# Reads of transposed probabilities moved from SyncE's queue to ScalarE's, in an attention and MLP kernel

## The chip, the cores and the metric

The kernel runs on one core of a Trainium2 chip. The metric is the device time of one execution in microseconds (us). The core has five engines with an instruction queue each: TensorE (PE in the profile; its weight loads are PEld), VectorE (DVE), ScalarE (ACT), GpSimd (POOL) and SyncE (SP). Each takes its own instructions strictly in order; they meet through semaphores. SP and ACT can also issue DMAs, which run on 16 DMA engines.

## The reference

```python
# 8 batches, 8 heads, 576 positions, head size 64
scores = q @ k.transpose(0, 1, 3, 2) / sqrt(64)
rel = pos[:, None] - pos[None, :]
slopes = 2.0 ** (-8.0 * (arange(8) + 1) / 8)
mask = (rel >= 0) & (rel < 128)
scores = where(mask, scores - slopes * abs(rel), -1e9)
attn = exp(scores - max(scores)); attn /= sum(attn) + 1e-9
x = (attn @ v)                      # then laid out as [4608 tokens, 512]
out = relu(x @ w_in) ** 2 @ w_out   # w_in 512 x 2048, w_out 2048 x 512
```

Attention with a sliding window of 128 positions feeds a two-layer MLP. All is float32; the MLP's products are made of high and low parts in a rounded format (fp32r), three matmuls for one.

## The kernel before

The 4608 tokens are nine chunks of 512 (`c`), each with four pairs of heads (`p`). A pair of heads of a chunk is a `Couple` (number `q`), made of two `Segment`s of 256 tokens (number `k`, from 0 to 71). A first part of the program (`start`) loads and converts the weights and does segments 0 to 15 and the MLP of the first chunk. Then `middle` does the rest. From some 250 us on, the first MLP layer uses Strassen-like sums of weights: seven products `M1, M5, M6, M2, M7, M3, M4` for two blocks (step number `n`). Their weights were written to HBM as `ws` between 137 and 250 us and are streamed back as tiles named `flow`. The second layer (`part`, line 388, `acc`) fills the room between them. PE's order is written out by hand.

Into this order 28 "visits" are put, one for each couple. A visit (`Visit`) does on PE: `one` and `two`, which multiply the previous couple's probabilities with the values (line 743, tile `pp`), and between them `scores` of the new couple (line 756).

Between two visits the new couple goes through softmax, segment by segment: copies and masks (`base`, `fold`), maxima (`t`, line 422), exponentials on ACT (`e`, line 429), sums, normalization on POOL (`norm`, line 441, tile `t`). Then the probabilities must be transposed. `Segment.squares` does so in four steps, which carry the change:

- `square` (line 493): DVE transposes squares of 32 x 32 into the tile `pp`.
- `write` (line 497): SP issues four DMAs of 64 KB that put the squares into a DRAM tile `way`.
- `read` (line 502): SP waits until the writes have landed and issues one DMA of 256 KB that reads `way` back into `pp` in the order wanted.
- `before` and `same` (line 508): POOL waits for the read and masks the two halves with `affine_select`.

The visit that uses the couple starts with `one`, which waits for `same` of both segments. Its second half `two` also waits for a no-operation on POOL (line 760). So a segment is late for its visit if this line of square, write, read and masks ends after PE gets there.

All loads, stores of results (`send`), streams of weight sums (`flow`) and spills of weight sums (`ws`) go through `bulk` (line 123) on SP's queue, as do `write` and `read`. For segments 16 to 27 (`k < CALM`), `read` leaves its DMA in `K.quiet`, and the next `bulk` then waits until that read has landed.

The order of the instructions on all engines but PE comes from a planner (`Plan`) when the program is built. Each step has an engine, an estimated duration, predecessors, a due time, and a `lag` that is added after its predecessors. The planner walks through a model of time and takes the ready step with the lowest due time. A step handed over from SP counts 2.0 us more, one from ACT 0.15. `DUE` holds the due times and `LAG` lags of the weight sums' steps. In the model, `quiet` and `calm` (2.4 us) hold bulk transfers after a read.

The drains of the seven products gate PE: `M6` waits for `s1` (ACT, line 339), `M2` for `R` (ACT, line 341), `M7` for `s2` (ACT, line 343), and the next `M1` needs the bank that `C21` (ACT, line 351) empties.

Of the kernel before, what the change touches and what calls it, by code (L numbers as in the profile page):

```python
# [55 lines left out]
CALM = 28  # L56
# [8 lines left out]
class Kern:  # L65
# [251 lines left out]
    def chain(self):  # L317
        if "one" not in self.open:
            self.banks("one", "two")
        self.P = self.pools[0].tile([128, 512], F32, name="chain")[:, 0:256]  # L320

# [11 lines left out]
    def seven(self, n):  # L333
# [3 lines left out]
        return {  # L337
            "M1": lambda: (self.chain(), self.product(n, 0, self.P, "B11", True)),
            "s1": lambda: nc.scalar.copy(four[0][:, one], self.P),
            "M5": lambda: (self.rest(), self.product(n, 1, self.R, "T1", True)),  # L340
            "R": lambda: nc.scalar.copy(four[1][:, two], self.R),
            "M6": lambda: self.product(n, 2, self.P, "T2"),
            "s2": lambda: nc.scalar.copy(four[0][:, two], self.P),
            "M2": lambda: self.product(n, 3, self.Q, "B21"),
            "C11": lambda: add(four[0][:, one], self.Q),
            "M7": lambda: self.product(n, 4, self.P, "T3"),
            "C22": lambda: add(four[1][:, two], self.P),
# [63 lines left out]
class Segment:  # L411
# [76 lines left out]
    def squares(self):  # L488
        nc = self.nc
        self.place()  # L490
        at = lambda x, pattern: x.rearrange("p m c -> p (m c)").rearrange(pattern, m=4, c=32)
        squares = at(self.prev, "p (b m c) -> p b m c")
        nc.vector.transpose(squares.rearrange("p b m c -> p m b c"), self.t.rearrange("p m (b c) -> p m b c", c=32))
        yield
        way = self.K.dr.tile([128, 512], F32, name="way")
        for a in range(4):
            nc.sync.dma_start(
                way.rearrange("(b r) (a f) -> a r b f", r=32, a=4)[a],
                squares[32 * a : 32 * a + 32].rearrange("r b m c -> r b (m c)"),
            )  # L500
        yield
        made = nc.sync.dma_start(self.own.rearrange("p m c -> p (m c)"), way)
        if self.K.calm and self.k < CALM:
            self.K.quiet = made
        self.own, self.prev = (at(x, "p (a m c) -> p a m c") for x in (self.own, self.prev))
        for to, sign, op in ((self.prev, 1, ALU.is_gt), (self.own, -1, ALU.is_ge)):
            yield
            nc.gpsimd.affine_select(  # L508
                to, self.own, pattern=[[-32 * sign, 4], [0, 4], [-sign, 32]], compare_op=op, fill=0.0,
                base=0, channel_multiplier=sign,  # L510
            )
# [327 lines left out]
class Plan:  # L839
# [5 lines left out]
    def add(self, name, engine, us, after, due, do, take=None, free=None, lag=0):  # L845
        rooms = lambda r: (r,) if isinstance(r, str) else r or ()
        assert name not in self.steps, name
        self.steps[name] = (engine, us, after, due + NUDGE.get(name, 0), do, rooms(take), rooms(free), lag)
# [64 lines left out]
def start(K):  # L913
# [109 lines left out]


ACT, DVE, POOL = "Activation", "DVE", "Pool"
LAG = {"a0": 5, "r0": 1, "s2": 5.5, "h0": 2.5, "l0": 0.5, "w0": 1.5}
DUE = {
    "wait": (0.3, 1), "give": (-49.7, -45.4, -56.8, -41.1), "send": (-5.5,), "load": (57.9, 14.5), "fill": (4.1, 12.2),
    "base": (-95.4, -1.6), "fold": (14.4, 18.6), "t": (-148.1, -124.5), "e": (17.7, -22), "sum": (-74.4, -18.5),
    "norm": (-66.5, -66.6), "square": (30.1, -17.8), "first": (-800, -48.8, 17.5, -51.6),  # L1030
    "ws": (25.9, 40.9, 61, 100.6, 76, 70.4, 79.8, 124.2), "flow": (30, 32.6), "sq": (26, 47.2), "high": (-48.4, -45.6),
    "hl": (-116.2, -92.7), "early": (73.8, 75.3, 94.3, 88.6, 30.9, 76.9),
    "third": (40.7, 35.4, 25.2, 18.2, -9.2, 3.5, 49.5, 31.9, 9.4, 18.2, -0.2, 26.2),
    "last": (-6.5, -34.8, -6.1, 24.6, -34.4, -48, -21.5, 14.7, -26.2, -11.8, -33.6, -11.8),
}
SOFT = dict(M1=0.72, g=0.7, first=2.79, one=0.85, scores=0.75, two=0.65)
PIECES = ("M1", "M5", "M6", "M2", "M7", "M4", "M3")
# [6 lines left out]


def middle(K, waiting):
    P = Plan(DUE["wait"][0], ("t", "ws"), DUE["wait"][1], 4.3, 2.4)
    for name, n in (
        ("one", 1), ("two", 1), ("s", 1), ("t", 1), ("pp", 2), ("qk", 2), ("v", 1), ("o", 4), ("hh", 1), ("r", 1),
    ):  # L1050
# [2 lines left out]
    now, last = 0.0, ()  # L1053

    def pe(name, us, after, fn, take=None, free=None):
        nonlocal now, last
        P.add(name, "PE", us, tuple(after) + last, now, fn, take, free)
        now, last = now + us, (name,)
        return now
# [15 lines left out]
    def chain(q, s, V):  # L1075
        G, k = waiting[q].both[s], 2 * q + s
        n = lambda a, *m: (a, k, *m)
        for m in range(4):
            P.add(n("t", m), DVE, 0.22, (n("t", m - 1) if m else n("fold"),), V + DUE["t"][s], do(G.top, m))
            P.add(n("e", m), ACT, 0.4, (n("t", m),) + ((n("e", m - 1),) if m else ()), V + DUE["e"][s], do(G.exp, m))  # L1080
        P.add(n("sum"), DVE, 0.38, (n("e", 3),), V + DUE["sum"][s], G.sums)
        P.add(n("norm"), POOL, 1.1, (n("sum"),), V + DUE["norm"][s], G.norm)
        turned(q, s, V + DUE["square"][s], (n("norm"),))

    def turned(q, s, d, after):
        G, k = waiting[q].both[s], 2 * q + s
        n = lambda a, *m: (a, k, *m)
        step = do(next, G.squares(), None)
        P.add(n("square"), DVE, 0.72, after, d, step, "pp", "t")
        P.add(n("write"), "SP", 1.8, (n("square"),), d - 500, step)  # L1090
        P.add(n("read"), "SP", 0.7, (n("write"),), d - 500, step, None, None, 2)
        P.add(n("before"), POOL, 0.81, (n("read"),), d - 500, step)
        P.add(n("same"), POOL, 0.81, (n("before"),), d - 500, step)

    def visit(q):
# [52 lines left out]
    for s in range(2):  # L1148
        turned(8, s, 4.0 + 3 * s, ())
    for n in range(NF, 2 * NF):  # L1150
        g = K.gemm1(*divmod(n, NF))
        step = lambda g=g: next(g, None)
        if n == NF:
            second(2)
        t = pe(("first", n), SOFT["first"], (), step, ("one", "two"))
# [8 lines left out]
        if n % 2:  # L1164
# [3 lines left out]
            step = lambda g=g: next(g, None)  # L1168
            w = lambda a: ("ws", j, a)
            d = t + DUE["ws"][j]  # L1170
            after = (("first", n),)
            early = (("first", max(NF, n - 5)),)
# [4 lines left out]
            before = ()  # L1177
            for name, engine, us, after in todo:
                lag = LAG.get(name, 0)
                P.add(  # L1180
# [3 lines left out]
                before = (w(name),)  # L1184
# [22 lines left out]
    for n in range(NF, FULL):  # L1207
        c, j = divmod(n, 8)
# [5 lines left out]
        for names, count in zip((("M1",), ("M5", "M6"), ("M2", "M7"), ("M3", "M4")), counts):  # L1214
            for m in names:
# [3 lines left out]
                t = pe((m, n), SOFT["M1"], after, steps[m], {"M1": "one", "M5": "two"}.get(m))  # L1219
# [12 lines left out]
        for f in range(2):  # L1232
            g = K.squared(n, f)
            step = lambda g=g: next(g, None)
# [22 lines left out]
@with_exitstack  # L1257
def tile_attn_moe(ctx: ExitStack, tc: tile.TileContext, *aps):
    K = Kern(ctx, tc, *aps)
    K.const()  # L1260
    with tc.manual_schedule(engines={ENGINES["PE"]}):
        with tc.manual_schedule(engines={e for n, e in ENGINES.items() if n != "PE"}):
            start(K)
            K.join(ctx)
            K.rooms()
            middle(K, {8: K.pairs[8]})
# [58 lines left out]
```

## Time and the profile before

| | |
|---|---|
| median of 3 runs | 915.62 us (913.82 to 916.09) |
| profiled execution | 915.75 us, of which the profile's span is 914.0 us |
| granted TensorE clock | 0.999 |
| PE busy | 903.4 us, 99% of the span |
| weight loads busy | 800.5 us, 88% |
| DVE, ACT, POOL busy | 581.8, 467.0, 260.2 us |
| DMA | 212.95 MB, 233 GB/s in the mean |
| DMA issues of the four steps | 256 writes `way<-pp` of 64 KB, 64 reads `pp<-way` of 256 KB, all on SP |

Busy time is the share in which an engine executes. For PE it is modelled from the starts of matmuls, so the idle time that the waits show is the safer measure. A row of waits names who waited, for whom, the total, the number of times and the longest. The time of a DMA "to landing" is counted from its issue.

### The profile page before, as it was taken

What the parts mean: (1) busy time and instruction counts of PE and PEld (TensorE: products, weight loads), DVE (VectorE), ACT (ScalarE), POOL (GpSimd) and SP (SyncE); (2) the same over time, 40 slices, a digit from 0 to 9 for tenths busy, and PEclk for the clock granted to TensorE, in tenths of its full rate; (3) what the DMA queues carried; (4) which work ended last, traced back from release to release, by engine and by line L of the source; (5) the groups of instructions that cost most, each with busy time, mean ns of one, the idle gap of its engine ahead of it and who ended that gap; (6) DMA issues with size and microseconds to landing.
All of it is one profiled execution on the core that took longest, in us unless ns stands there. A gap on an engine that the chain in (4) does not pass through costs nothing.

```text
span 914.0 us, 23218 instructions
## 1 busy us (share of the span) xinstructions
PE 903.4 (99%) x8500; PEld 800.5 (88%) x8500; DVE 581.8 (64%) x1596; ACT 467.0 (51%) x1321; POOL 260.2 (28%) x339
## 2 busy tenths in 40 slices
PE   8999999999999999999999999999999999999998
PEld 5688888888899998999999999999999989989997
DVE  6999882667776666665656665667666566653333
ACT  7898663566554445444544444445444454432222
POOL 4213335665422322213222322231322221230000
PEclk9999999999999999999999999999999999999999
DMA  9985326768888878777877778777977786667541
GB/s 343 403 313 171 88 62 218 236 215 270 292 285 297 295 248 283 233 237 239 256 236 246 245 242 290 233 230 213 294 231 221 245 248 192 197 208 221 172 127 47
DMA packets 137569, 212.95 MB, mean 233 GB/s; under 512 B 15217, under 2 KB 49393, under 8 KB 137457
## 3 DMA queue, kind: packets, MB, share of 16 engines
q1 hardware_dynamic: 137024, 210.96, 71.1%
q8 instruction: 68, 1.11, 0.5%
q10 hardware_dynamic: 432, 0.52, 0.2%
q14 instruction: 45, 0.36, 0.1%
HBM read 170.52 MB, written 40.89 MB: 231 GB/s over the span
## 4 chain that ended last, share of the span: by engine, by line
PE 90%; DMA 7%; DVE 1%; POOL 1%; ACT 1%; SPq 1%; issue 0%; POOLq 0%; DVEq 0%; ACTq 0%
PE acc L388 42%; PE chain L331 16%; PE rest L331 12%; PE g L233 9%; PE s L743 5%; PE g L756 2%; DMA raw<-in_dram 2%; DMA pp<-way 1%; PE s L756 1%; DMA qk<-in_dram 1%; DMA flow<-ws 1%; PE at L520 1%; POOL pp L508 1%; DMA wide<-in_dram 1%; DMA out_dram<-o 0%
## 5 line engine op out<-in xcount | busy, mean ns | idle before, releaser
L388 PE MATMUL acc<-hh,w 128*128 128x512 f32 x1152 | 405.8, 398 | 0.0
L388 PEld LDWEIGHTS acc<-hh,w 128*128 128x128 f32 x1152 | 225.8, 196 | 39.3 <-issue 5.5
L388 PE MATMUL acc<-hl,w 128*128 128x512 f32 x576 | 227.7, 395 | 0.0
L336 DVE TENSOR_TENSOR four<-four,rest 128x256 f32<-128x256 f32 x112 | 47.2, 421 | 215.6 <-PE rest L331 214.5
L508 POOL TENSOR_SCALAR_AFFINE_SELECT pp<-pp 128x512 f32<-128x512 f32 x128 | 96.6, 757 | 223.8 <-DMA pp<-way 134.6
L331 PEld LDWEIGHTS rest<-xu,flow 128*128 128x128 f32 x1008 | 143.9, 191 | 13.0
L351 ACT COPY four<-chain 128x256 f32<-128x256 f32 x56 | 20.9, 373 | 251.6 <-PE chain L331 251.6
L331 PE MATMUL chain<-tees,flow 128*128 128x256 f32 x1008 | 147.6, 283 | 0.0
L331 PE MATMUL rest<-xu,flow 128*128 128x256 f32 x1008 | 146.8, 282 | 0.0
L441 POOL TENSOR_TENSOR t<-t,nm 128x512 f32<-128x512 f32 x64 | 69.5, 1089 | 239.4 <-DVE nm L437 152.1
L331 PEld LDWEIGHTS chain<-tees,flow 128*128 128x128 f32 x1008 | 132.3, 192 | 0.0
L388 PEld LDWEIGHTS acc<-hl,w 128*128 128x128 f32 x576 | 113.1, 196 | 12.6
L429 ACT ACTIVATE t<-t,nm 128x128 f32<-128x128 f32 x256 | 100.3, 394 | 9.4 <-DVE nm L422 8.8
L233 PE MATMUL g<-xu,w 128*128 128x512 f32 x384 | 95.3, 397 | 0.8 <-ACT r L242 0.8
L233 PEld LDWEIGHTS g<-xu,w 128*128 128x128 f32 x384 | 76.5, 210 | 13.8 <-ACT r L242 1.2
L422 DVE CUSTOM_DVE_ANT_0 t<-t,cst 128x128 f32<-128x128 f32 x256 | 63.1, 303 | 1.7
L251 DVE TENSOR_TENSOR hl<-r,hh 128x512 fp32r<-128x512 f32 x32 | 29.1, 910 | 42.3 <-ACT hh L249 42.2
L743 PE MATMUL s<-pp,v 64*64 64x128 f32 (+1 forms) x1792 | 53.6, 248 | 1.8 <-POOL pp L508 1.6
L656 DVE COPY_PREDICATED t<-cst,s 64x256 f32<-64x256 int32 x100 | 44.5, 445 | 12.6 <-PE s L743 5.8
L331 PEld LDWEIGHTS chain<-xu,flow 128*128 128x128 f32 x336 | 48.7, 196 | 4.0
L331 PE MATMUL chain<-xu,flow 128*128 128x256 f32 x336 | 49.4, 284 | 0.0
L429 ACT ACTIVATION_READ_ACCUMULATOR t<-t,nm 128x1 f32 x256 | 48.3, 189 | 0.0
(106 smaller groups left out, 1135.5 us busy)
## 6 DMA issues: line engine op xcount, KB each, us to landing
flow<-ws SPq DMA_DIRECT2D x392, 256.0 KB, 4.1
raw<-in_dram SPq DMA_DIRECT2D x32, 512.0 KB, 8.7
way<-pp SPq DMA_DIRECT2D x256, 64.0 KB, 2.1
pp<-way SPq DMA_DIRECT2D x64, 256.0 KB, 2.9
qk<-in_dram SPq DMA_DIRECT2D x32, 320.0 KB, 4.7
v<-in_dram SPq DMA_DIRECT2D x32, 320.0 KB, 3.6
qk<-in_dram SPq DMA_DIRECT2D x38, 256.0 KB, 5.0
out_dram<-o SPq DMA_DIRECT2D x35, 256.0 KB, 3.5
```

Source lines behind the costliest of these rows:

```text
L233: nc.tensor.matmul(g, w, xs[cc][:, part], start=i == 0, stop=i == 11)
L251: nc.vector.tensor_tensor(hl, r, hh.bitcast(F32), op=ALU.subtract)
L331: self.nc.tensor.matmul(to, w, x, start=start and k == 0, stop=k == 5, skip_group_check=True)
L336: add = lambda to, x: nc.vector.tensor_tensor(to, to, x, op=ALU.add)
L388: self.nc.tensor.matmul(self.acc[m], w, h, start=(f == 0 and i == 0), stop=(f == NF - 1 and i == 2))
L422: self.nc.vector.tensor_tensor_reduce(self.t[:, m], self.t[:, m], self.K.nrel(2 * self.p + m // 2), -0.125, BIG, ALU.add, ALU.min, self.nm ...
L429: return self.nc.scalar.activation(self.t[:, m], self.t[:, m], AF.Exp, bias=nm[:, 4 + m : 5 + m], scale=-1.0, accum_out=nm[:, m : m + 1],)
L441: self.nc.gpsimd.tensor_tensor(*(x.rearrange("p (j i) c -> p j i c", j=2) for x in (self.t, self.t)), self.rec.unsqueeze(3).to_broadcast([ ...
L508: nc.gpsimd.affine_select(to, self.own, pattern=[[-32 * sign, 4], [0, 4], [-sign, 32]], compare_op=op, fill=0.0, base=0, channel_multiplie ...
L656: nc.vector.copy_predicated(d, mask.unsqueeze(1).to_broadcast([64, 2, 2, 64]), e)
L743: yield self.nc.tensor.matmul(to, w, x, start=first and n < 2, stop=not first, skip_group_check=True)
L756: made = self.nc.tensor.matmul(to, w, x, start=not extra, stop=True, skip_group_check=True)
```

## The change

Three things. In `middle`, `read` is issued on ACT's queue; `start` keeps SP's. No read is left in `K.quiet`, so no bulk transfer waits for one. The planner's figures are new: `read` is an ACT step of 0.45 us with a lag of 1 us behind `write`, `before` has a lag of 2.4 us behind `read`, and nearly all due times and weight-sum lags differ.

```diff
@@ Segment.squares
-        made = nc.sync.dma_start(self.own.rearrange("p m c -> p (m c)"), way)
-        if self.K.calm and self.k < CALM:
-            self.K.quiet = made
+        queue = nc.scalar if self.K.calm else nc.sync
+        queue.dma_start(self.own.rearrange("p m c -> p (m c)"), way)
@@
-LAG = {"a0": 5, "r0": 1, "s2": 5.5, "h0": 2.5, "l0": 0.5, "w0": 1.5}
+LAG = {"a0": 6.5, "r0": 1.5, "s2": 4, "h0": 3, "l0": 0, "w0": 0}
 DUE = {
-    "wait": (0.3, 1), "give": (-49.7, -45.4, -56.8, -41.1), "send": (-5.5,), "load": (57.9, 14.5), "fill": (4.1, 12.2),
-    "base": (-95.4, -1.6), "fold": (14.4, 18.6), "t": (-148.1, -124.5), "e": (17.7, -22), "sum": (-74.4, -18.5),
-    "norm": (-66.5, -66.6), "square": (30.1, -17.8), "first": (-800, -48.8, 17.5, -51.6),
+    "wait": (0.3, 1), "give": (26.5, -41.3, -5.4, -21.2), "send": (-34.5,), "load": (15.5, -24.2), "fill": (-14, 18.9),
+    "base": (-67.8, -7.9), "fold": (33.1, -23.5), "t": (-141, -100), "e": (24.9, 28.8), "sum": (-60.6, -26.8),
+    "norm": (-105.2, -55.8), "square": (-10.8, -0.6), "first": (-800, -43, 44.3, -36.7),
...
 }
@@ middle
-    P = Plan(DUE["wait"][0], ("t", "ws"), DUE["wait"][1], 4.3, 2.4)
+    P = Plan(DUE["wait"][0], ("t", "ws"), DUE["wait"][1], 4.3)
@@ turned
         P.add(n("write"), "SP", 1.8, (n("square"),), d - 500, step)
-        P.add(n("read"), "SP", 0.7, (n("write"),), d - 500, step, None, None, 2)
-        P.add(n("before"), POOL, 0.81, (n("read"),), d - 500, step)
+        P.add(n("read"), ACT, 0.45, (n("write"),), d - 500, step, None, None, 1)
+        P.add(n("before"), POOL, 0.81, (n("read"),), d - 500, step, None, None, 2.4)
         P.add(n("same"), POOL, 0.81, (n("before"),), d - 500, step)
```

The diff leaves out the other due times (`ws`, `flow`, `sq`, `high`, `hl`, `early`, `third`, `last`), which change by up to some 105 us of the planner's scale. PE's order is the same before and after.

More of the change, by code (lines that the diff above doesn't have):

```diff
@@ L1025 @@
 ACT, DVE, POOL = "Activation", "DVE", "Pool"
-LAG = {"a0": 5, "r0": 1, "s2": 5.5, "h0": 2.5, "l0": 0.5, "w0": 1.5}
+LAG = {"a0": 6.5, "r0": 1.5, "s2": 4, "h0": 3, "l0": 0, "w0": 0}
 DUE = {
-    "wait": (0.3, 1), "give": (-49.7, -45.4, -56.8, -41.1), "send": (-5.5,), "load": (57.9, 14.5), "fill": (4.1, 12.2),
-    "base": (-95.4, -1.6), "fold": (14.4, 18.6), "t": (-148.1, -124.5), "e": (17.7, -22), "sum": (-74.4, -18.5),
-    "norm": (-66.5, -66.6), "square": (30.1, -17.8), "first": (-800, -48.8, 17.5, -51.6),
[L1031 to L1034, printed above, removed]
+    "wait": (0.3, 1), "give": (26.5, -41.3, -5.4, -21.2), "send": (-34.5,), "load": (15.5, -24.2), "fill": (-14, 18.9),
+    "base": (-67.8, -7.9), "fold": (33.1, -23.5), "t": (-141, -100), "e": (24.9, 28.8), "sum": (-60.6, -26.8),
+    "norm": (-105.2, -55.8), "square": (-10.8, -0.6), "first": (-800, -43, 44.3, -36.7),
+    "ws": (52.1, 52.8, 39.9, 104.3, 72.2, 74.5, 100.5, 130.1), "flow": (40.8, 46), "sq": (32.9, 20.6),
+    "high": (-112.3, -150.4), "hl": (-140.6, -122.4), "early": (58, 64.9, 63, 75.9, 48.3, 28.3),
+    "third": (75, 43.4, 37.9, 27.6, 3.4, 32, 74.1, 39.6, 11.3, 37.8, 10.5, 35.8),
+    "last": (29.7, 16.4, 29.2, 69.1, 11.7, -4, -8.1, 32.3, 1.2, 18.8, -2.1, 38.5),
 }
```

## Prediction

> **What bounds the kernel now.** I read the page first, for the engine that is full and the chain that ended last.
>
> ```profile
> PE   903.4 (99%) x8500; PEld 800.5 (88%) x8500; DVE 581.8 (64%) x1596; ACT 467.0 (51%) x1321; POOL 260.2 (28%) x339
> PE 90%; DMA 7%; DVE 1%; POOL 1%; ACT 1%; SPq 1%; issue 0%; POOLq 0%; DVEq 0%; ACTq 0%
> ```
>
> PE is full, and 90% of the chain is PE. So the change, which leaves PE's instructions and their order alone, can win only what PE idles, and can lose by making it idle more. The windows of the part that the change touches (columns: window, its length, then busy us of PE, PEld, DVE, ACT and POOL with instruction counts, clock, DMA share, GB/s) show how little that is:
>
> ```profile
> 236.00:256.00 20.00, 20.00 (x125) 18.28 (x125) 15.84 (x50) 12.18 (x38) 7.09 (x11) 1.00 0.74 231
> 256.00:353.00 97.00, 96.94 (x1024) 88.41 (x1023) 62.81 (x184) 46.64 (x149) 25.77 (x37) 1.00 0.86 282
> 353.00:450.00 97.00, 96.67 (x1013) 88.16 (x1013) 61.69 (x181) 46.09 (x142) 26.38 (x38) 1.00 0.78 245
> 450.00:741.00 291.00, 290.78 (x3067) 265.38 (x3065) 182.91 (x543) 137.62 (x431) 77.72 (x109) 1.00 0.78 247
> 741.00:816.00 75.00, 73.90 (x815) 67.26 (x813) 45.73 (x132) 34.02 (x108) 20.07 (x26) 1.00 0.67 213
> ```
>
> From 236 to 816 us PE idles 0.06 + 0.33 + 0.22 + 1.10 = 1.7 us. Then the waits of PE and of its weight loads, since a weight load stands ahead of its matmul and takes the wait first:
>
> ```profile
> PE s L743 <- POOL pp L508: 1.6, 3, 1.1
> PEld s L743 <- POOL pp L508: 2.3, 4, 1.2
> PEld s L743 <- POOLq L760: 0.4, 1, 0.4
> ```
>
> Four of 28 visits find POOL's masks (line 508) late, for 2.3 us in all, 1.2 in the worst; a fifth waits 0.4 for POOL's no-operation. The first two rows are the same four waits seen twice. So 2.3 + 0.4 = 2.7 us can be removed, and nothing else on PE depends on the reads: no row of waits has line 331 (the streams) or line 388 waiting for ACT or a DMA.
>
> Now the worst visit, at 741.2 us: the end of the square on DVE, SP's queue, POOL, ACT, PE (start, length).
>
> ```profile
> 730.36 0.70 DVE L493 STREAM_TRANSPOSE pp<-t 128x512 f32<-128x512 f32 x1
> ```
> ```profile
> 729.68 3.70 SPq L497 DMA_DIRECT2D way<-pp  x8
> 733.56 0.34 SPq L502 DMA_DIRECT2D pp<-way  x1
> 733.94 0.91 SPq L123 DMA_DIRECT2D out_dram<-o  x2
> 735.02 0.34 SPq L502 DMA_DIRECT2D pp<-way  x1
> 735.41 1.07 SPq L123 DMA_DIRECT2D out_dram<-o  x2
> 736.52 5.72 SPq L123 DMA_DIRECT2D flow<-ws  x8
> ```
> ```profile
> 736.54 1.52 POOL L508 TENSOR_SCALAR_AFFINE_SELECT pp<-pp 128x512 f32<-128x512 f32 x2 [6.62 <-DMA pp<-way]
> 740.73 1.84 POOL L508 TENSOR_SCALAR_AFFINE_SELECT pp<-pp 128x512 f32<-128x512 f32 x2 [2.67 <-DMA pp<-way]
> ```
> ```profile
> 734.99 0.37 ACT L341 COPY four<-rest 128x256 f32<-128x256 f32 x1 [0.17 <-PE rest L331]
> 735.70 0.37 ACT L343 COPY four<-chain 128x256 f32<-128x256 f32 x1 [0.34 <-PE chain L331]
> 741.36 0.37 ACT L351 COPY four<-chain 128x256 f32<-128x256 f32 x1 [5.29 <-PE chain L331]
> ```
> ```profile
> 742.62 0.89 PE L743 MATMUL s<-pp,v 64*64 64x64 f32 x29 [1.10 <-POOL pp L508]
> ```
>
> The second segment decides: its square ends at 731.06, its masks at 742.57, 11.5 us later, and PE resumes at 742.62. Of that the read's landing is the largest piece, issue at 735.02 to the masks at 740.73, 5.7 us. Two other visits just make it:
>
> ```profile
> 545.81 1.52 POOL L508 TENSOR_SCALAR_AFFINE_SELECT pp<-pp 128x512 f32<-128x512 f32 x2 [1.22 <-DMA out_dram<-o]
> 642.37 1.52 POOL L508 TENSOR_SCALAR_AFFINE_SELECT pp<-pp 128x512 f32<-128x512 f32 x2 [1.06 <-DMA pp<-way]
> ```
> ```profile
> 547.67 0.56 PE L743 MATMUL s<-pp,v 64*64 64x64 f32 x16
> 644.18 0.62 PE L743 MATMUL s<-pp,v 64*64 64x64 f32 x20
> ```
>
> Masks end at 547.33 and 643.89, so each has 0.3 us left. These six are the visits, from the fourth chunk on, that use a chunk's first pair of heads (segments 24 and 25, then every eighth). So every us by which the masks come later costs about 4 us at the four late visits and 0.7 each at these two, 5.4 us; every tenth earlier pays back at most 0.4, one tenth at each of four.
>
> **The change part by part.**
>
> *The read leaves SP.* SP no longer stops for the writes to land or, for segments 16 to 27, for the read to land:
>
> ```profile
> SPq L502 <- DMA way<-pp: 19.3, 30, 4.3
> SPq L123 <- DMA pp<-way: 15.9, 6, 3.4
> ```
>
> SP is freed of up to 35 us. Nothing on PE waits for SP's transfers, so this is worth 0 by itself; what covers it is that streams are issued well ahead of their products. But the freed SP issues its next sends and streams while the writes are still landing: at the visit above two sends and the first streams (735.41 on) can go ahead of the read instead of behind it. The first segment's read no longer queues behind the second's four writes; that moves only the first pair of masks (736.54), which does not decide: 0.
>
> *How long writes and reads then take to land.* The rows to bound it: reads of the stretch 137 to 243 us, where bulk transfers are held, and reads and writes from 360 us on, where they follow at once (min/median/max).
>
> ```profile
> L502 SPq DMA_DIRECT2D pp<-way x8: 338/338/338, 144.1 to 223.3; - x8
> DMA to landing us min/median/max: 2.5/2.7/3.0
> ```
> ```profile
> L502 SPq DMA_DIRECT2D pp<-way x38: 319/338/380, 367.4 to 808.1; - x38
> DMA to landing us min/median/max: 2.5/3.4/5.6
> ```
> ```profile
> L497 SPq DMA_DIRECT2D way<-pp x152: 302/430/1701, 363.5 to 805.8; - x152
> DMA to landing us min/median/max: 1.6/2.1/4.3
> ```
>
> Transfers issued behind a read on the same queue already cost it 3.4 - 2.7 = 0.7 us. With them ahead, and in another queue, no row shows it: from -0.7 (as if alone) to +2.2 for the read (5.6 - 3.4), and 0 to +2.2 for the write (4.3 - 2.1). I take +0.2 for both together, nearest to no change, since the same bytes share the same engines in the same few us, only in another order. The 12 reads that lose their hold get at most the 0.7; the visits from 158 to 233 us have no waits on PE and cover it.
>
> The Trainium skill ("DMA: Bandwidth & Descriptors", section "Queues, rings and completion order") says that each DMA engine takes turns between the queues it has work for, so a read in a queue of its own would not stand behind what SP queued; by that it keeps near the 2.7. The same page, "Issuing engines are not separate DMA queues", says that all queues end on the same 16 engines and only issue time is saved; by that it stays at 3.4 or more. The trace has no read on ACT's queue to decide.
>
> *The read joins ACT.* An issue there costs what the two ACT issues at the start of the program took:
>
> ```profile
> 0.81 0.44 ACTq L148 DMA_DIRECT2D wide<-in_dram  x1
> 1.28 0.45 ACTq L138 DMA_DIRECT2D cst<-in_dram  x1
> ```
>
> 56 reads of 0.44 are 25 us of ACT's queue, beside 51% busy: no bound. Per read it is +0.1 over SP's 0.34. Position: ACT is in order, so at the worst visit the read starts after the copy that ends at 735.36 or after the next at 736.07, against 735.02 on SP: +0.3 or +1.05. Before the copy of 741.36 ACT idles 5.29 us; put behind that one the read would be 6 us late, which I leave to a rival. I take +0.4 with the issue, the earlier place, since the planner puts it by time. Queued behind the waiting read are drains and casts, and PE waits for the drains. Their cover is the second layer between the products:
>
> ```profile
> 263.02 1.40 PE acc L388 x6
> ```
>
> Between a product and the one that needs its drain stand 1.40 us of this and another product (six matmuls, 0.72 in the planner's table), 2.1 less a copy of 0.37. ACT may thus stand 1.7 us for a landing before PE notices. The planner counts 3.0 us from the end of the writes' issue to the read, above the 2.1 median landing, so ACT mostly arrives late and does not stand: 0, up to +0.5 a visit if a landing takes the 4.3 and the drains follow.
>
> *The plan.* Planned from square to masks, the line was 1.8 + 2 + 0.7 + 2.0 = 6.5 us and is 1.8 + 2.0 + 1 + 0.45 + 0.15 + 2.4 = 7.8, 1.3 longer and nearer to the trace. With dues to match, squares can come up to 1.3 us earlier at the late visits. Bounds -1.3 (all fits) and 0 (DVE, busy 62.81 of 97 us in the first of these windows, has no room there); new dues can also leave another segment late, up to the +1.2 that is the longest wait now. I take -1.0.
>
> *Other dues and the weight sums' lags.* They move work that PE does not wait for (20.00 of 20.00 busy from 236 to 256): 0, covered by those margins.
>
> **Sum.** Position +0.4, landing +0.2, plan -1.0: masks 0.4 us earlier. The waits (1.2 the longest, three sharing 1.1) then keep about 0.9 of 2.3, and the no-operation's 0.4 stays: 1.4 us gained. The profiled execution took 915.75 (914.0 of span and 1.75 around it), 0.13 above the median of 915.62: 915.75 - 1.4 = 914.4.
>
> **Rivals.**
> - *All waits go.* The reads land as if alone and the squares come earlier: -2.7, 913.05. For it: four waits of at most 1.2 us against a plan that adds 1.3. Against: the same transfers share the engines. The skill's rule of turns between queues leads here: 0.7 earlier at each late visit leaves 0.5 of the longest wait.
> - *The read is late behind bulk transfers.* What SP held back goes out ahead of it. If masks come 1.0 us later, +5.4: 921.2; it decides from about 0.5 later (4 x 0.5 + 2 x 0.2 = 2.4, 918.2). For it: the landing rows (median up 0.7 from transfers merely behind, worst 5.6) and three positions on ACT that are all later than SP's. Against: the plan's 1.3.
> - *The read lands behind a drain.* A single visit of 28 with the read planned close to the copy that waits for PE (5.29 us idle) costs up to 6 us: 914.4 + 6 = 920.4. For it: ACT's long waits just ahead of the visits. Against: the planner's model knows PE's times well, as the few waits show.
> - *The move changes nothing.* The visits keep their waits: 915.7.
>
> **How the numbers follow.** A measurement here can tell about 0.3%, 2.75 us, so 912.87 to 918.37 is no difference. The forecast with its own range of 913.0 to 917.0 has 0.42, no change 0.10, all waits gone 0.25, reads late 0.18, a read behind a drain 0.05. All waits gone (913.05) stands 0.18 above the edge; the runs of before reach 1.80 below their median and 0.47 above, so I count six in ten of it as faster, 0.15, and 0.03 from the forecast's low end. Of the late reads and the drain 0.21 lie past the upper edge. So faster 0.18, same 0.61, slower 0.21. The range of 912.6 to 919.0 leaves out the worse half of the late reads and little below.
>
> **What would show it.** Right: reads on ACT's queue, no row of SP waiting at line 502 after 137 us, a sum of waits of line 743 for line 508 of about 1 us, reads landing at a median of 3.2 to 3.8. Wrong: that sum above 4 us, or waits of PE for ACT's copies (lines 339, 341, 343, 351), which are absent now; or reads at a median above 4.5.

## The result and the profile after

The changed kernel takes 944.06 us (median of 4 runs), the kernel before 915.49: a ratio of 1.032 (95% interval 1.0281 to 1.0358). The forecast was 914.4, with a range of 912.6 to 919.0. The profiled execution took 941.67 us, 939.8 of it span, 25.8 more than the span before.

In the code below `squares` has one line less, so the masks have line 507 (508 before), the read line 503 (502) and the visit's products line 742 (743). From the page, the engines' busy time and the chain that ended last:

```profile
PE 910.6 (97%) x8500; PEld 805.4 (86%) x8500; DVE 594.9 (63%) x1596; ACT 467.9 (50%) x1321; POOL 266.5 (28%) x339
PE 82%; DMA 10%; POOL 2%; DVE 2%; ACT 1%; issue 1%; SPq 1%; ACTq 0%; POOLq 0%; DVEq 0%
```

PE's share of the chain fell from 90% to 82%. The waits of PE and of its weight loads (total, times, longest) say for what:

```profile
PE s L742 <- POOL pp L507: 19.2, 9, 2.7
PEld s L742 <- POOL pp L507: 20.9, 11, 2.8
```

Before, the second row was 2.3 us in 4 waits. The visits now wait 18.6 us more for the masks. The reads themselves, all 40 from 360 us on, on ACT's queue (min/median/max):

```profile
L503 ACTq DMA_DIRECT2D pp<-way x40: 326/327/359, 359.7 to 833.0; - x40
DMA to landing us min/median/max: 2.8/5.0/6.0
```

They land 5.0 us after their issue instead of 3.4. Here is the visit that stood at 741.2 us before, of the same two segments: SP, ACT, POOL, PE, DVE.

```profile
753.13 3.72 SPq L497 DMA_DIRECT2D way<-pp  x8
756.95 0.39 SPq L123 DMA_DIRECT2D out_dram<-o  x1
757.44 0.39 SPq L123 DMA_DIRECT2D flow<-ws  x1
757.92 0.89 SPq L123 DMA_DIRECT2D out_dram<-o  x2
758.90 0.45 SPq L123 DMA_DIRECT2D flow<-ws  x1
759.45 0.82 SPq L123 DMA_DIRECT2D out_dram<-o  x1
760.36 5.03 SPq L123 DMA_DIRECT2D flow<-ws  x5
```
```profile
758.04 0.37 ACT L341 COPY four<-rest 128x256 f32<-128x256 f32 x1 [0.17 <-PE rest L331]
758.27 0.33 ACTq L503 DMA_DIRECT2D pp<-way  x1
758.75 0.37 ACT L343 COPY four<-chain 128x256 f32<-128x256 f32 x1 [0.34 <-PE chain L331]
759.21 0.33 ACTq L503 DMA_DIRECT2D pp<-way  x1
```
```profile
762.31 1.52 POOL L507 TENSOR_SCALAR_AFFINE_SELECT pp<-pp 128x512 f32<-128x512 f32 x2 [8.62 <-DMA pp<-way]
765.19 2.02 POOL L507 TENSOR_SCALAR_AFFINE_SELECT pp<-pp 128x512 f32<-128x512 f32 x2 [1.35 <-DMA out_dram<-o]
```
```profile
764.25 0.33 PE L742 MATMUL s<-pp,v 64*64 64x64 f32 x2
767.26 0.89 PE L742 MATMUL s<-pp,v 64*64 64x64 f32 x29 [2.69 <-POOL pp L507]
```
```profile
765.53 1.09 DVE L365 TENSOR_TENSOR hl<-r,hh 128x512 fp32r<-128x512 f32 x1
766.54 1.19 DVE L365 TENSOR_TENSOR hl<-spare,hh 128x512 fp32r<-128x512 f32 x1
```

The writes' issue ends at 756.85. SP does not stop any more: sends and streams go out from 756.95 on, so several large transfers are in flight when ACT, held by its copies for PE, issues the second read at 759.21. Its masks start at 765.19, 6.0 us later, when PE has been there for 0.9 us. And then they take 2.02 us instead of 1.52, beside the two DVE operations shown.

The line from the square to the visit can be put together from such rows for every segment. Medians of the 24 second segments from number 25 on, in us; "ahead" is the mean number of large transfers that SP issued in the 3 us before the read:

| kernel | writes issued | landed | to read's issue | read lands | masks end | square to visit | margin | ahead |
|---|---|---|---|---|---|---|---|---|
| before | 2.50 | 1.33 | 0.31 | 4.02 | 1.72 | 11.75 | 1.95 | 1.8 |
| changed | 2.52 | 1.36 | 1.32 | 5.57 | 1.92 | 12.44 | 0.04 | 4.5 |

The squares do come 0.7 us earlier. Against this stand 1.0 us until ACT issues the read, 1.55 in its landing and 0.2 in the masks. The margin falls from 1.95 to 0.04, so about half of the visits are late.

What makes a read slow can be read from the kernel before already, when for each read the large transfers are counted that SP had issued and that had not landed (called in flight) at the read's issue. Of the 48 reads from segment 24 on, 22 are issued with none in flight and land in 2.72 us (median), though 3.5 large transfers on average are issued behind them before they land; 22 have two in flight and land in 4.07. At the visit of 741.2 us, which the prediction shows, the read at 733.56 has none in flight and lands in 2.87 us; the one at 735.02 has the two sends of 733.94 in flight and lands in 5.57. In the changed kernel second segments' reads have 4.75 in flight on average, against 1.83 before.

Most of the rest of the loss is the clock. Windows (busy us of PE, PEld, DVE, ACT, POOL, then granted clock, DMA share, GB/s):

```profile
256.00:350.00 94.00, 86.64 (x923) 78.68 (x922) 55.87 (x149) 38.87 (x122) 24.18 (x32) 0.95 0.75 247
350.00:475.00 125.00, 119.62 (x1260) 108.90 (x1259) 79.25 (x234) 58.14 (x182) 32.29 (x45) 1.00 0.75 239
475.00:764.00 289.00, 285.21 (x2928) 260.30 (x2927) 180.67 (x530) 133.57 (x421) 77.64 (x106) 1.00 0.75 241
```

From 256 to 350 us the mean clock is 0.95 instead of 1.00: it was 0.50 from 260.5 to 267.3 us and from 342.4 to 345.8 us, 10.2 us in all, of which half is lost, some 5.1 us. Waits and clock make 18.6 + 5.1 = 23.7 of the 25.8 us; where the remaining 2 us lie is not shown.

### The profile page after: what moved, and what is told of

The parts are those of the page before. It is cut to its first block, busy times and chain, and to the rows that moved or that the text cites. A ratio compares the mean times of both kernels' runs of the same rounds, so it can differ in the third digit from the quotient of the medians.

```text
span 939.8 us, 23305 instructions
## 1 busy us (share of the span) xinstructions
PE 910.6 (97%) x8500; PEld 805.4 (86%) x8500; DVE 594.9 (63%) x1596; ACT 467.9 (50%) x1321; POOL 266.5 (28%) x339
## 4 chain that ended last, share of the span: by engine, by line
PE 82%; DMA 10%; POOL 2%; DVE 2%; ACT 1%; issue 1%; SPq 1%; ACTq 0%; POOLq 0%; DVEq 0%
PE acc L388 39%; PE chain L331 14%; PE rest L331 11%; PE g L233 9%; PE s L742 5%; DMA pp<-way 4%; PE g L755 2%; POOL pp L507 2%; DMA raw<-in_dram 2%; DMA cst<-in_dram 2%; DMA flow<-ws 2%; PE s L755 1%; PE at L519 1%; DMA way<-pp 1%; DMA out_dram<-o 1%
## 5 line engine op out<-in xcount | busy, mean ns | idle before, releaser
L507 POOL TENSOR_SCALAR_AFFINE_SELECT pp<-pp 128x512 f32<-128x512 f32 x128 | 102.0, 798 | 292.4 <-DMA flow<-ws 110.5
L351 ACT COPY four<-chain 128x256 f32<-128x256 f32 x56 | 20.9, 373 | 252.6 <-PE chain L331 231.5
L742 PE MATMUL s<-pp,v 64*64 64x128 f32 (+1 forms) x1792 | 58.7, 255 | 19.5 <-POOL pp L507 19.2
L422 DVE CUSTOM_DVE_ANT_0 t<-t,cst 128x128 f32<-128x128 f32 x256 | 67.1, 317 | 1.7
L742 PEld LDWEIGHTS s<-pp,v 64*64 64x64 f32 x1792 | 45.3, 138 | 25.9 <-POOL pp L507 20.9
```

The costliest lines, as they stand in the source:

```text
L422: self.nc.vector.tensor_tensor_reduce(self.t[:, m], self.t[:, m], self.K.nrel(2 * self.p + m // 2), -0.125, BIG, ALU.add, ALU.min, self.nm ...
L507: nc.gpsimd.affine_select(to, self.own, pattern=[[-32 * sign, 4], [0, 4], [-sign, 32]], compare_op=op, fill=0.0, base=0, channel_multiplie ...
L742: yield self.nc.tensor.matmul(to, w, x, start=first and n < 2, stop=not first, skip_group_check=True)
```

## The experiments

Each ratio is against the kernel before on the same chip.

### The due times alone, and the queue alone

The due times and lags of the changed kernel put into the kernel before:

```diff
-LAG = {"a0": 5, "r0": 1, ...}; DUE = {...}      # old
+LAG = {"a0": 6.5, "r0": 1.5, ...}; DUE = {...}  # new; reads on SP, old planner steps, old hold
```

> The new due times and weight-sum lags, but the reads on SP with the planner's old figures and the old hold for segments 16 to 27. Queue theory (the reads are late because they left SP's queue, where they went ahead of the streams): reads land at a median of about 3.4 us as before, the waits of the visits for the masks stay under 5 us, time 913 to 919. Due-time theory (the new order makes the masks late whatever the queue): waits near the 20.9 us of the changed kernel, 935 or more.

925.09 us, 1.0102 (1.0067 to 1.0136): between the theories. Weight loads of the visits wait twice as long as before, and one stream comes late (a row of PE):

```profile
PEld s L743 <- POOL pp L508: 4.6, 4, 1.2
PE rest L331 <- DMA flow<-ws: 3.7, 1, 3.7
```

The reverse, the changed kernel with the old `LAG` and `DUE`:

> The old due times and lags, but the reads on ACT's queue with the planner's new figures and no hold. Queue theory: reads land at a median of 4.5 to 5.5 us, waits for the masks 15 us or more, time 930 to 950. Due-time theory: 914 to 920, waits under 5 us.

952.72 us, 1.0412 (1.0372 to 1.0452). The queue theory holds in direction, at more than its range:

```profile
PEld s L742 <- POOL pp L507: 21.4, 9, 4.0
PE chain L331 <- DMA flow<-ws: 6.8, 2, 6.3
DMA to landing us min/median/max: 2.6/4.7/7.0
```

So the new due times cost 1.0% on SP, and on ACT the kernel is faster with them than with the old ones, which here also bring a stream 6.3 us late. The larger part of the loss comes with what was done to the reads.

### Holding the large transfers again

In the changed kernel the next large transfer waits for the last write of a segment:

```diff
-            nc.sync.dma_start(way..., squares...)
+            made = nc.sync.dma_start(way..., squares...)
+        if self.K.calm:
+            self.K.quiet = made
```

> The changed kernel, but the next large transfer on SP waits until a segment's last write has landed, which gives back the stop that SP made there for the read. If the lost stop is the cause (streams go out between the writes and the read): reads land at 3.4 to 4.2 us, waits for the masks under 10 us, 918 to 930. If reads on a queue of their own land late whoever went first, or ACT issues them late: over 935.

938.54 us, 1.0226 (1.017 to 1.0281), above the range and with runs from 929.75 to 940.49; second segments' reads land in 4.52 us. Waits for the masks halve, but new ones appear, for ACT's drains (a row of PE):

```profile
PEld s L744 <- POOL pp L509: 10.8, 7, 2.8
PE chain L331 <- ACT four L343: 4.3, 2, 3.4
```

Now the hold behind each read:

```diff
-        queue.dma_start(self.own..., way)
+        made = queue.dma_start(self.own..., way)
+        if self.K.calm:
+            self.K.quiet = made
```

> The changed kernel, but the next large transfer on SP after each read waits until that read has landed; transfers between the writes and the read still go ahead. If transfers issued behind the read take its share of the engines: reads land at 3 to 4 us and the waits fall by half or more, 915 to 930, unless the held streams come late themselves (then PE waits at line 331). If only those ahead of it matter: reads stay at 4.5 us or more, over 935.

923.73 us, 1.0086 (1.0059 to 1.0113). This takes back 20 of the 28.6 us:

```profile
PEld s L744 <- POOL pp L509: 5.3, 3, 2.8
DMA to landing us min/median/max: 2.6/3.4/5.2
```

In second segments the landing falls from 5.57 to 3.31. This does not single out transfers behind a read: those held behind the first segment's read are also missing ahead of the second's, which has 2.0 in flight instead of 4.75. Both holds together:

> The changed kernel with both holds: the next large transfer waits for a segment's last write, and again for its read, to land. If transfers ahead of the read and transfers behind it add up (the first hold took 1.05 us off the second segments' landing of 5.57, the second 2.26): reads land at 2.2 to 2.7 us, and the waits for the masks fall below the 5.3 us of the hold behind the read; 916 to 928, the rest being ACT's later issue and streams or drains that are held up. If the two do not add: landing stays at 3.3 or more.

935.95 us, 1.0194 (1.0168 to 1.0221). They do not add; second segments land at 4.26 and the waits are 15.2 us. A transfer that is held for the write's landing goes out when that landing releases ACT's read too, so it meets the read. The rows bear this out: 1.5 large transfers on average go out between that landing and a second segment's read, 0.1 with the hold behind the read alone. No run tests it by itself.

### Fewer bytes beside the reads

```diff
-        self.bulk(self.flow[n % 2][i].bitcast(F32), self.sums[n % 8][:, i])
+        a = 512 if n < NF + 2 else 256
+        self.bulk(self.flow[n % 2][i][:, :a].bitcast(F32), self.sums[n % 8][:, i, :a])
```

> The changed kernel, but from the third step on a stream loads only the first half of its weight sums (128 KB instead of 256), so part of the products is computed with old data. If the reads are late for the bytes that the engines carry beside them: reads land at 3 to 4 us, waits for the masks under 8 us, 917 to 930. If a queue of its own is slow whatever the load, or ACT's position is the cause: landing 4.5 us or more, over 935.

936.09 us, 1.0204 (1.0183 to 1.0224), between the two. The reads land at a median of 3.6 us from 360 us on, so bytes matter; the second segments' 4.37 is still above the 4.02 of before, and the waits are 14.6 us.

### An earlier place on ACT

```diff
-        P.add(n("read"), ACT, 0.45, (n("write"),), d - 500, step, None, None, 1)
+        P.add(n("read"), ACT, 0.45, (n("write"),), d - 500, step, None, None, -1.5)
```

> The changed kernel, but the planner puts the read 0.5 us after the writes' issue instead of 3.0, so it stands earlier in ACT's order. If ACT's position costs the 1.0 us by which reads start later after the landing than on SP: that falls from 1.3 us to 0.3 to 0.6, the masks come about 0.8 us earlier, waits of 12 to 18 us, 930 to 941. If ACT standing for the landing holds up the drains: PE waits for lines 339 to 351 and the time is 945 or more.

944.05 us, 1.0315 (1.0285 to 1.0346): the time of the changed kernel, for another reason. From the landing of the writes to the read's issue it takes 0.10 us instead of 1.32, and waits for the masks fall from 20.9 us to 4.4. But ACT stands for the landing, and PE for ACT; two streams come late as well (the last two rows, of PE):

```profile
PEld s L742 <- POOL pp L507: 4.4, 5, 1.2
PEld chain L331 <- ACT four L339: 7.0, 10, 1.2
PEld acc L388 <- ACT o L399: 4.0, 4, 1.5
PEld chain L331 <- ACT four L351: 3.0, 5, 1.7
PE chain L331 <- DMA flow<-ws: 3.8, 1, 3.8
PE rest L331 <- DMA flow<-ws: 2.8, 1, 2.8
```

On ACT a read is late behind copies, or the copies are late behind the read.

### The hold for all reads, on SP and on ACT

The kernel before with one constant changed:

```diff
-CALM = 28
+CALM = 72
```

> The kernel before, but the hold of large transfers on SP goes for all reads and not for segments 16 to 27 alone (CALM = 72), in the planner's model too. If transfers behind the read are what delays it on SP as well: reads land at 2.3 to 3.0 us instead of 3.4, the four waits for the masks go, 912.5 to 914.5. If the held streams then come late for their products: PE waits at line 331, 917 to 930.

912.93 us, 0.9953 (0.9937 to 0.9968): 0.5% faster than the kernel before, inside the first theory's range. From 360 us on:

```profile
PEld s L743 <- POOL pp L508: 2.1, 1, 2.1
DMA to landing us min/median/max: 2.5/2.7/4.8
```

Second segments' reads have no large transfer in flight at their issue, land in 2.83 us instead of 4.02, and their margin is 3.05. One wait is left, near 257 us. The same plan and order, with the queue alone changed:

```diff
+CALM = 72
-        made = nc.sync.dma_start(self.own..., way)
+        made = (nc.scalar if self.K.calm else nc.sync).dma_start(self.own..., way)
```

> The kernel before with the hold for all reads (CALM = 72), its plan and order kept, and only the queue of the reads changed from SP to ACT. Nothing large is in flight beside the reads that were issued after them. If the queue itself costs nothing: reads land at 2.5 to 3.0 us as with the same on SP. SP no longer stops for the writes, so transfers ahead of the read can still go: then 3.0 to 3.8. If ACT standing for the landing costs: PE waits for drains (lines 339 to 351), 915 to 930; if not, 912 to 916.

919.33 us, 1.0028 (1.0002 to 1.0055). No weight load waits for masks any more, and reads land as on SP, but drains are late:

```profile
L502 ACTq DMA_DIRECT2D pp<-way x38: 326/326/371, 368.6 to 810.9; - x38
DMA to landing us min/median/max: 2.5/2.7/3.5
PEld chain L331 <- ACT four L351: 4.9, 4, 1.8
```

So ACT's queue neither slows nor speeds a read that has the engines for itself (2.67 us in second segments, 2.83 on SP). The ratios are 0.9953 and 1.0028; the new waits for ACT are the largest difference that the rows show.

### The plan, and the missing hold

The changed kernel with its plan, its reads issued on SP at the same places:

```diff
-        queue = nc.scalar if self.K.calm else nc.sync
+        queue = nc.sync
```

> The changed kernel with its plan and order, but the reads' DMAs are issued on SP at the same place of the program, with no hold. SP then stops for the writes' landing again and sends what stands behind the read in its own order only after it. If the lost stop and ACT's place in the order are the loss: second segments' reads land at 3.8 to 4.6 us and start within 0.5 us of the writes' landing, waits for the masks under 8 us, 918 to 930. If the plan, which counts the reads as ACT's, is the loss: over 935.

941.95 us, 1.0288 (1.0265 to 1.031). The first theory fails: without ACT, and with SP's stop for the writes back, the loss is still there. The plan's order by itself puts 3.8 large transfers into the 3 us ahead of a second segment's read, and the read starts 1.24 us after the writes have landed.

```profile
PEld s L742 <- POOL pp L507: 20.2, 10, 3.2
DMA to landing us min/median/max: 2.7/4.5/5.8
```

The old due times on ACT with the hold after each read:

> The old due times, the reads on ACT's queue, and the next large transfer on SP after each read held until it has landed. Against the same without the hold (952.7, second segments' landing 5.4, waits 21.4): if transfers beside the read make it late under either set of due times, the landing falls to 3.0 to 3.8 us, the waits under 8 us, 918 to 932. If the hold helped only with the new due times: over 940.

932.5 us, 1.0179 (1.015 to 1.0208). Landing (3.50 in second segments) and waits for masks (4.3 us) are as expected, so the hold works under either set of due times; the time is just above the range, with 8.1 us of waits for two late streams (6.8 without the hold).

The third part of the change alone, `CALM = 0` in the kernel before:

> The kernel before with the hold taken away for segments 16 to 27 too (CALM = 0), in the planner's model as well; reads stay on SP, old due times. This is the change's third part alone. If the hold matters where it stands: the reads before 250 us land later (2.7 to 3.4 or more), and with them one or two visits; 916 to 920. If it is covered by the margins of those visits: 914.5 to 916.5.

926.32 us, 1.0103 (1.0071 to 1.0135): far over both ranges, and not by late masks (1.7 us):

```profile
PE chain L331 <- DMA flow<-ws: 6.6, 2, 5.4
256.00:350.00 94.00, 88.58 (x955) 80.48 (x954) 56.15 (x165) 42.41 (x136) 24.02 (x33) 0.96 0.82 265
```

The hold also shapes the planner's order where the streams begin, near 250 us. Without it one stream comes 5.4 us late, and the mean clock of this stretch is 0.96. The run with the old due times on ACT, which has no hold either, has a stream 6.3 us late.

Two last runs divide the 17 us between 925.1 (new due times on SP) and 942.0 (the same due times, new planner figures, no hold). New due times on SP with `CALM = 0`:

> The new due times, the reads on SP with the planner's old figures (an SP step of 0.7 us, 2 us after the writes), and no hold at all. It stands between the same with the hold for segments 16 to 27 (925.1) and the changed plan with its reads issued on SP (942.0). If the planner's figures for the read are what puts streams ahead of it: 922 to 932, waits for the masks under 8 us. If the missing hold is: 936 to 944, waits over 15 us.

928.36 us, 1.0137 (1.0101 to 1.0172), second segments landing at 4.54 with 2.0 transfers ahead, waits 8.2 us. So some 14 us are the planner's figures for the read (1.0137 against 1.0288); the 3 us left for the hold lie within the intervals. Taken one after the other, the parts of the change give 1.0102 (due times), 1.0137 (no hold), 1.0288 (planner's figures) and 1.032 (ACT's queue); the first and the third step are clear of their intervals, the other two are not. And the changed kernel with the old hold given back:

> The changed kernel with the old hold for segments 16 to 27 given back, in the planner's model too; the reads stay on ACT. If the hold is a part by itself (worth 9.5 us with the old due times on SP): 932 to 938. If it acts through SP's queue alone: 941 to 947.

943.52 us, 1.0318 (1.0283 to 1.0353): nothing gained, as the last line of the expectation has it.

## Why the prediction was wrong

- *What bounds the kernel* was right: PE's work is unchanged and PE loses only by waiting at the visits. The price per us of lateness came from six visits; at 1.9 us some thirteen are late, so it rises faster than the 5.4 that I used.
- *How long reads take to land* is the step that failed. I had bounds of -0.7 to +2.2 and took +0.2 for reads and writes together, "nearest to no change, since the same bytes share the same engines". Second segments' landing rose by 1.55, while the writes' stayed (1.33 and 1.36). What mattered was what is in flight when the read is issued: 1.8 large transfers in the 3 us ahead of it before, 4.5 after. I priced SP's freedom at 0, and saw the transfers move ahead, but gave that no time. The price was in the rows, misread: I put 3.4 - 2.7 = 0.7 down to transfers issued behind a read. The median of 3.4 mixes first segments' reads, at 2.72 with almost nothing in flight, with second segments', at 4.02 with 1.8. From 2.72 and 4.07 a transfer in flight ahead costs some 0.7 us; 2.9 more of them would have given +2.0 (an estimate), near the +1.55 measured.
- *The read leaves SP* had its 35 us too large: 13.3 of the 19.3 us for the writes lie ahead of 137 us, in `start`, whose reads stay on SP, and from 260 us on that stop takes 2.1 us in 7 waits. So the stop itself held back little where the visits are late. Given back, with the reads on SP in the changed plan, it brings the time only to 941.95.
- *Position on ACT* was +0.4 and is +1.0, the later of the two places that I worked out (+1.05). Behind it lies the step that I did not see as a cost at all: the planner's new figures. They count the read 3.0 us after the writes and take it off SP's time, so the planner fills SP with streams in between. On SP, without a hold and with the same due times, the new figures take 941.95 us and the old ones 928.36.
- *The plan*, -1.0, was nearly right: squares come 0.7 us earlier, 1.1 at the six visits (10.14 to 11.21).
- *The missing hold* was priced at 0, since it touches 12 reads with wide margins. With the old due times it costs 9.5 us alone, mostly through a late stream, which the margins of the reads do not cover; with the new due times no cost is clear of the intervals.
- *ACT's standing* at 0 was right for the changed kernel only because ACT came late; put earlier, PE waits 14.0 us for it in the three rows shown.
- The rival "late behind bulk transfers" is what happened, at 1.9 us instead of the 1.0 that gave 921.2. Its chance of 0.18 was too low: the row of landing times spoke for it, and I let the planner's 1.3 us outweigh it.
- On the Trainium skill ("DMA: Bandwidth & Descriptors"): turns between queues ("Queues, rings and completion order") did not shield the read. With the engines free it lands in 2.7 us on either queue; in the changed plan in 4.88 on SP, with 4.0 large transfers in flight, and in 5.57 on ACT, with 4.75. The sentence that queues share the same 16 engines ("Issuing engines are not separate DMA queues") agrees with this. With four in flight the medians, over all reads from segment 24 on, are 5.02 on SP (18 reads) and 4.93 on ACT (8 reads), so no cost of ACT's queue itself shows in the landing; the intervals of the ratios 1.0288 and 1.032 overlap.

## What to carry to other kernels

When a transfer changes its queue or its place in a plan, count what will be in flight when it is issued. In these kernels a read with nothing large in flight landed in 2.7 to 2.9 us even with several large transfers issued behind it, and each one in flight ahead added 0.5 to 0.7 us ((5.57 - 2.87) / 5 in the changed kernel, from its reads with none and with five in flight, and (4.07 - 2.72) / 2 before). A plan that takes a step off one queue fills the room that is left, here with streams ahead of the read. Where a short transfer is on the critical line, the gain was in holding the large ones until it had landed (0.9953 for one constant), not in a queue of its own; and an engine whose copies gate the bottleneck is a poor place for a DMA that must wait.

## What was not expected of the hardware

In the changed kernel eleven masks beside the DVE operations of lines 358 and 365 take 1.0 to 1.3 us each instead of 0.73, and the subtractions of line 365 beside a mask 1.08 to 1.19 instead of 0.69; masks beside line 336 alone keep their 0.73. The two masks at 765.19 above took 2.02 us, beside the two subtractions shown. A pair of masks that meets them thus loses some 0.5 us more. The Trainium skill ("SBUF — State Buffer", section "SBUF: two separate sides") has DVE operations with two inputs in SBUF and GpSimd share a pair of ports; these rows agree with it.

Some stalls cost a second time. In the changed kernel PE waited 2.7 us until 261.4 and 2.1 us until 342.1, and the granted clock was 0.50 from 260.5 to 267.3 and from 342.4 to 345.8. Waits of 2.7 us later (767.26) left it at 1.00; what decides is not shown.
